# A fused attention and gated MLP kernel on one core: attention by 256-token steps over all heads in place of whole sequences by head pair

## The chip, the cores and the metric

The kernel runs on one core of a Trainium2 chip. A core has a matrix engine (TensorE, "PE" in the profile, with "PEld" for its weight loads), a vector engine (VectorE, "DVE"), a scalar engine (ScalarE, "ACT"), a general engine (GpSimd, "POOL") and a queue engine that here only issues transfers (SyncE, "SP"). Each engine works through its own list of instructions in order and waits for the others by semaphores. Data come from device memory (HBM) by 16 DMA engines into SBUF; TensorE writes to PSUM, from where VectorE or ScalarE carry results back to SBUF ("eviction"). The metric is the time of one execution in microseconds (us), lower is better.

## The reference

`x` is the attention's output with the heads side by side; shapes are batch 4, 8 heads, 768 tokens, head size 64, model width 512, MLP width 1024.

```python
# attention, for each block of 64 tokens, state kv_state (64 x 64 per head) starts at 0
intra = einsum('bhic,bhjc->bhij', qb, kb) * Dmask      # lam**(i-j) for i >= j, else 0
intra = einsum('bhij,bhjd->bhid', intra, vb)
inter = einsum('bhid,bhde->bhie', qb * lam_pow, kv_state)
out[:, :, sl] = intra + inter
kv_state = lam_block * kv_state + einsum('bhsd,bhse->bhde', kb * rev_pow, vb)
# gated MLP on x (4, 768, 512)
h = maximum(x @ w_in, 0);  u, v = h[..., :512], h[..., 512:]
v_n = (v - mean(v)) / sqrt(var(v) + 1e-6)              # over the 512 features
v_s = einsum('ts,bsd->btd', w_spatial, v_n) + b_spatial
out = (u * v_s) @ w_out
```

Inputs and output are fp32; q, k and v have 6.29 MB each, the output 6.29 MB, w_in 2.10, w_spatial 2.36, w_out 1.05 MB. Of `v_s` every token of a batch needs all 768 tokens' `v_n`, so the second half of the MLP starts when the first is done for the batch.

## The kernel before

Attention is computed in blocks of 128 tokens. The state's and the mask's powers of `lam` are put into the operands: k is cast to bf16 and scaled per head (`kd`, by `ldec`), the transposed q is scaled on eviction (`qT`, by `lq`), and the scores are scaled by a causal mask (`a`, by `amask`).

The work around attention is cut into *units*: unit u is one batch and one pair of heads (g), over all 768 tokens, 16 units in all. A unit has five parts: `cast_unit` (kd on ScalarE, qc on VectorE for batch 0 and on GpSimd after, vc on GpSimd), `trans_unit` (12 transposes into one PSUM tile `pt`, evicted as kT by ScalarE and qT by VectorE), `scores_unit` (12 matmuls into two tiles `pam`, each evicted by VectorE with the mask), `kv_unit` (10 matmuls into `pkv`, then a chain of one copy and four multiply-adds on VectorE that makes the five states `s`), and `out_unit` (10 matmuls with the state and 12 with the scores into `pat`, evicted by ScalarE into a fourth of `xT`, the MLP's transposed input).

The MLP of a batch is cut into *pieces* (`gmlp_pieces`): three `pv` (256 tokens of v each, with the normalization on VectorE), four `pu` (128 features of u, all tokens), four `pvs` (the product over tokens and the gate `gT`), three `po` (256 tokens of the output, evicted by ScalarE and stored). Since `xT` has all its rows only after the fourth unit, `pv` and `pu` of a batch come behind all four units.

All PSUM tiles come from one ring of four slots of two banks (`two_banks`), so a piece can start when the piece four places ahead of it is evicted. SBUF tiles come from pools with a number of buffers (`fin` for inputs: 2, each a whole batch).

The order on TensorE and GpSimd is that of the program text (`manual_schedule`); on the other engines a scheduler of the framework sets it when the kernel is built. The main loop interleaves: batch 0's units, then 11 of its MLP pieces; then for each further batch its units, with the pieces of the batch ahead put between them by `fill(n)`, which takes n pieces from the list `pend`. The last batch's MLP stands alone at the end.

Loads of q, k and v go through SP's queue: batch 0 by head pair (12 transfers), the others as three transfers a batch; those of batch 1 are issued at unit 2, and its k load is made to wait for the load of w_spatial (`after`). The weights are loaded by GpSimd's queue, cast to bf16 on the way. Stores of the output use SP's queue too.

Of the kernel before, what the change touches and what calls it, by code (L numbers as in the profile page):

```python
# [9 lines left out]
FP32 = mybir.dt.float32  # L10
BF16 = mybir.dt.bfloat16
# [7 lines left out]
def kernel(  # L19
# [21 lines left out]
    NU = B * NG  # L41
    HW_ = S // 2
    NPAIR = S // (2 * P)
# [3 lines left out]
    fin = ctx.enter_context(tc.tile_pool(name="fin", bufs=2))  # L47
# [4 lines left out]
    ostg = ctx.enter_context(tc.tile_pool(name="ostg", bufs=2))  # L52
# [9 lines left out]
    q_in, k_in, v_in = {}, {}, {}  # L62

    def alloc_in(b):
        q_in[b] = fin.tile([P, H, NPAIR, 2, D], FP32, tag="q_in", name=f"q_in_{b}")
        k_in[b] = fin.tile([P, H, NBLK, D], FP32, tag="k_in", name=f"k_in_{b}")
        v_in[b] = fin.tile([P, H, NBLK, D], FP32, tag="v_in", name=f"v_in_{b}")

    def load_q(b, h0, h1):
        return nc.sync.dma_start(  # L70
            out=q_in[b][:, h0:h1].rearrange("p h r m d -> p (h r) (m d)"),
            in_=q[b, h0:h1].rearrange("h (r p m) d -> p (h r) (m d)", p=P, m=2))

    def load_kv(dst, src, b, h0, h1):
        return nc.sync.dma_start(  # L75
            out=dst[b][:, h0:h1].rearrange("p h m d -> p (h m) d"),
            in_=src[b, h0:h1].rearrange("h (m p) d -> p (h m) d", p=P))

    def after(inst, gate, reason):
        tc.add_manual_dep(inst.ins, gate.ins.name,  # L80
                          mybir.DependencyInfo(mybir.DependencyClass.Sync,
                                               mybir.DependencyReason.DATA), reason=reason)

    def load_batch(b, gate=None):
        alloc_in(b)
        li = load_kv(k_in, k, b, 0, H)
        if gate is not None:
            after(li, gate, "earlier loads go first")
        load_q(b, 0, H)
        load_kv(v_in, v, b, 0, H)  # L90

    alloc_in(0)
    for g in range(NG):
        load_kv(k_in, k, 0, 2 * g, 2 * g + 2)
        load_q(0, 2 * g, 2 * g + 2)
        load_kv(v_in, v, 0, 2 * g, 2 * g + 2)
# [9 lines left out]


    qpos = iota_f([P, 2, 2, D], [[1, 2], [0, 2], [2, D]], 1, 0, "qpos")
    krev = iota_f([P, 1], [[0, 1]], P - 1, -1, "krev")
# [7 lines left out]
    wsp_raw = wpool.tile([P, NBLK, S], BF16)  # L117

# [9 lines left out]
    lq_g = []  # L128
    for g in range(NG):
        lq = const.tile([P, 2 * P], BF16, name=f"lq_{g}")  # L130
        nc.scalar.activation(out=lq, in_=qpos.rearrange("p m a d -> p (m a d)"), func=AF.Exp,
                             scale=logl[:, g:g + 1])
        lq_g.append(lq)
# [7 lines left out]
    amask = const.tile([P, H, P], FP32)  # L141
    for h in range(H):
        nc.vector.tensor_scalar(out=amask[:, h, :], in0=causal, scalar1=lm128[:, h:h + 1],
                                scalar2=None, op0=ALU.mult)
# [5 lines left out]
    def load_win(f0, f1):  # L150
        nc.gpsimd.dma_start(out=win_sb[:, :, f0:f1],
                            in_=moe_w_in.rearrange("(g p) f -> p g f", p=P)[:, :, f0:f1])


    xT = {}
    st = {}

    def cast_unit(u):
        b, g = divmod(u, NG)
        kd = att.tile([P, NBLK, 2, D], BF16, tag="kd", name=f"kd_{u}")  # L160
        qc = att.tile([P, NPAIR, 2, 2, D], BF16, tag="qc", name=f"qc_{u}")
        vc = att.tile([P, NBLK, 2, D], BF16, tag="vc", bufs=4, name=f"vc_{u}")
        for hh in range(2):
            h = 2 * g + hh
            nc.scalar.activation(out=kd[:, :, hh, :], in_=k_in[b][:, h], func=AF.Copy,  # L165
# [266 lines left out]
```

## Time and profile before

| | us |
|---|---|
| median of 3 executions | 197.62 |
| lowest, highest | 196.42, 197.75 |
| the profiled execution | 197.81 |
| its span, first to last instruction | 195.7 |

| engine | busy us | share of the span | instructions |
|---|---|---|---|
| PE | 154.7 | 79% | 1476 |
| PEld | 94.0 | 48% | 1476 |
| DVE | 103.8 | 53% | 252 |
| ACT | 94.9 | 48% | 130 |
| POOL | 31.5 | 16% | 70 |

The mean granted TensorE clock is 0.961 of full speed. The page gives the span in 40 slices of 4.89 us, a digit for the busy tenths of each engine in each; groups of instructions with their count, busy time, mean duration in ns and the idle time ahead of them with its releaser; and the DMA rate by slice. A row of a timeline has the start, the length from the first start to the last end, engine, line, operation, `out<-in`, shapes and count. Ends of matmuls are modelled, so two neighbouring rows overlap a little, and a price is best read from start to start.

### The profile page before, as it was taken

Reading aid. Unit: us, or ns where it says so; the run is one execution under the profiler, and the core shown is the slowest. Engines: PE = TensorE matmul, PEld = TensorE weight load, DVE = VectorE, ACT = ScalarE, POOL = GpSimd, SP = SyncE. Lnnn points to the kernel's source line nnn. Section 1 sums busy time; section 2 is a strip of 40 time slices with the busy share of each in tenths; the row PEclk is TensorE's granted clock in tenths of the full one; section 3 lists DMA queues with packets and bytes.
Section 4 is the critical chain, followed back from the end, with each engine's and each line's share of the span. In section 5 each row is a group of like instructions: output and inputs, shape, how many; then the busy total and the mean of one; then the engine's idle time right before and its main releaser. Section 6 shows DMA issues by size and latency. Waiting matters only on the chain.

```text
span 195.7 us, 3558 instructions
## 1 busy us (share of the span) xinstructions
PE 154.7 (79%) x1476; PEld 94.0 (48%) x1476; DVE 103.8 (53%) x252; ACT 94.9 (48%) x130; POOL 31.5 (16%) x70
## 2 busy tenths in 40 slices
PE   0046678999549999599589999976899999999980
PEld 0035565457225655355346655543566554466430
DVE  1448777094114767717995584059964830663300
ACT  3563542498463176736456542476463226670041
POOL 2124106102621015330223110030000000000000
PEclk9999999999987999859969999999999999999998
DMA  4999999999999997999910000430000005300034
GB/s 113 224 247 229 250 270 264 242 238 254 202 230 253 266 217 252 233 306 272 218 27 0 3 0 0 173 154 0 3 0 0 3 0 210 115 0 0 0 141 181
DMA packets 33151, 28.33 MB, mean 145 GB/s; under 512 B 13040, under 2 KB 27760, under 8 KB 33136
## 3 DMA queue, kind: packets, MB, share of 16 engines
q1 hardware_dynamic: 30480, 25.17, 51.7%
q0 software_dynamic: 2512, 2.95, 8.7%
q8 instruction: 11, 0.18, 0.4%
q14 instruction: 4, 0.03, 0.1%
q10 hardware_dynamic: 144, 0.00, 0.0%
HBM read 24.78 MB, written 6.29 MB: 159 GB/s over the span
## 4 chain that ended last, share of the span: by engine, by line
PE 47%; DMA 22%; DVE 13%; SPq 9%; ACT 6%; issue 2%; POOL 0%; ACTq 0%; DVEq 0%
PE pvs L303 16%; PE pu L292 8%; PE po L317 7%; DMA wsp_raw<-in_moe_w_spatial_dram 7%; DMA k_in<-in_k_dram 6%; DMA v_in<-in_v_dram 6%; SPq L75 5%; PE pv L273 4%; DVE a L214 4%; SPq L70 3%; DMA out_dram<-o 3%; PE pvs L305 3%; DVE gT L307 2%; DVE st L278 2%; PE pat L244 2%; PE pat L250 2%
## 5 line engine op out<-in xcount | busy, mean ns | idle before, releaser
L303 PE MATMUL pvs<-wt_sb,vn 128*128 128x384 bf16 x192 | 38.3, 336 | 3.2 <-ACT wt_sb L335 1.9
L253 ACT ACTIVATE xT<-pat 128x768 bf16<-128x768 f32 x16 | 16.5, 1030 | 34.5 <-PE pat L250 34.5
L214 DVE TENSOR_TENSOR a<-pam,amask 128x768 bf16<-128x768 f32 x32 | 29.4, 947 | 5.8 <-PE pam L211 5.8
L307 DVE TENSOR_TENSOR gT<-pvs,uT 128x768 bf16<-128x768 f32 x16 | 15.3, 957 | 24.7 <-PE pvs L305 24.7
L303 PEld LDWEIGHTS <-vn 128*128 128x128 bf16 x192 | 19.1, 100 | 16.1 <-issue 5.2
L292 PE MATMUL pu<-xT,win_sb 128*128 128x384 bf16 x128 | 23.6, 340 | 1.9 <-ACT xT L253 1.9
L273 PE MATMUL pv<-win_sb,xT 128*128 128x512 bf16 x96 | 24.3, 407 | 0.6 <-ACT vh L276 0.4
L171 POOL CAST vc<-v_in 128x384 bf16<-128x384 f32 x32 | 15.6, 515 | 52.2 <-DMA v_in<-in_v_dram 45.9
L278 DVE BATCH_NORM_STATS2 st<-vh 128x6 f32<-128x512 bf16 x24 | 15.7, 675 | 13.5 <-ACT vh L276 13.5
L317 PE MATMUL po<-wout_sb,gT 128*128 128x512 bf16 x96 | 21.9, 379 | 0.9 <-DVE gT L307 0.5
L190 DVE TENSOR_TENSOR qT<-pt,lq 128x768 bf16<-128x768 bf16 x16 | 8.8, 553 | 25.7 <-ACT kT L188 25.6
L320 ACT ACTIVATE o<-po 128x1024 f32<-128x1024 f32 x12 | 12.3, 1023 | 19.6 <-PE po L317 15.6
L165 ACT ACTIVATE kd<-k_in,ldec 128x384 bf16<-128x384 f32 x32 | 17.5, 603 | 7.7 <-DMA k_in<-in_k_dram 4.2
L181 PE MATMUL pt<-ident,kd 128*128 128x128 bf16 x96 | 9.6, 247 | 14.7 <-ACT kd L165 14.7
L211 PE MATMUL pam<-qT,kT 64*128 64x128 bf16 x192 | 9.4, 238 | 12.7 <-DVE qT L190 12.7
L188 ACT ACTIVATE kT<-pt 128x768 bf16<-128x768 bf16 x16 | 12.9, 807 | 12.5 <-PE pt L184 12.5
L230 DVE SCALAR_TENSOR_TENSOR s<-s,l,pkv 128x64 bf16<-128x64 bf16 x64 | 17.8, 279 | 1.8
L169 POOL CAST qc<-q_in 128x384 bf16<-128x384 f32 x24 | 11.6, 510 | 44.6 <-PE pt L184 27.4
L292 PEld LDWEIGHTS <-win_sb 128*128 128x128 bf16 x128 | 12.7, 101 | 10.8 <-issue 3.4
L276 ACT ACTIVATE vh<-pv 128x1024 bf16<-128x1024 f32 x12 | 12.3, 1022 | 9.1 <-PE pv L273 9.1
L211 PEld LDWEIGHTS <-kT 64*128 64x128 bf16 x192 | 7.3, 103 | 17.4 <-issue 9.6
L181 PEld LDWEIGHTS <-kd 128*128 128x128 bf16 x96 | 7.3, 110 | 17.3 <-ACT kd L165 15.1
(51 smaller groups left out, 155.3 us busy)
## 6 DMA issues: line engine op xcount, KB each, us to landing
out_dram<-o SPq DMA_DIRECT2D x12, 512.0 KB, 3.0
k_in<-in_k_dram SPq DMA_DIRECT2D x4, 384.0 KB, 6.4
q_in<-in_q_dram SPq DMA_DIRECT2D x4, 384.0 KB, 6.1
v_in<-in_v_dram SPq DMA_DIRECT2D x4, 384.0 KB, 6.4
wsp_raw<-in_moe_w_spatial_dram POOLq DMA_DIRECT2D x1, 1152.0 KB, 13.6
win_sb<-in_moe_w_in_dram POOLq DMA_DIRECT2D x2, 512.0 KB, 7.6
wout_sb<-in_moe_w_out_dram POOLq DMA_DIRECT2D x1, 512.0 KB, 17.2
bsp_bc<-in_moe_b_spatial_dram POOLq DMA_DIRECT2D x1, 192.0 KB, 14.1
```

The source lines that it names most:

```text
L165: nc.scalar.activation(out=kd[:, :, hh, :], in_=k_in[b][:, h], func=AF.Copy, scale=ldec[:, h:h + 1])
L181: nc.tensor.transpose(out=pk[:, m * P:(m + 1) * P], in_=kd[:, m].rearrange("p h d -> p (h d)"), identity=ident)
L211: nc.tensor.matmul(out=pam[:, hh, c, :], lhsT=kT[hh * D:(hh + 1) * D, t * P:(t + 1) * P], rhs=qblk(u, hh, t), start=True, stop=True)
L214: nc.vector.tensor_tensor(out=a_sb[:, :, 3 * i:3 * i + 3, :], in0=pam[:, :, 0:3, :], in1=amask[:, 2 * g:2 * g + 2].unsqueeze(2).broadcast_ ...
L230: nc.vector.scalar_tensor_tensor(out=s_sb[:, m], in0=s_sb[:, m - 1], scalar=l128[:, g:g + 1], in1=pkv[:, m], op0=ALU.mult, op1=ALU.add)
L253: nc.scalar.activation(out=xT[b][:, g, :].rearrange("p (c d m) -> p c m d", c=NBLK, m=2), in_=po[:, 0:NBLK].rearrange("p c (m d) -> p c m ...
L273: nc.tensor.matmul(out=ps[:, j], lhsT=x[:, c, t * P:(t + 1) * P], rhs=win_sb[:, c, DH:DFF], start=(c == 0), stop=(c == NCH - 1))
L278: nc.vector.bn_stats(out=st6[:, t, :], in_=vh[:, t, :])
L292: nc.tensor.matmul(out=ps[:, i, 0:HW_], lhsT=win_sb[:, c, f * P:(f + 1) * P], rhs=x[:, c, i * HW_:(i + 1) * HW_], start=(c == 0), stop=(c ...
L303: nc.tensor.matmul(out=ps[:, i, 0:HW_], lhsT=vn[:, s, f * P:(f + 1) * P], rhs=wt_sb[:, s, cols], start=(s == 0), stop=False)
L307: nc.vector.tensor_tensor(out=gT[:, f, :].rearrange("p (i x) -> p i x", i=2), in0=ps[:, :, 0:HW_], in1=uT[:, f, :].rearrange("p (i x) -> p ...
L317: nc.tensor.matmul(out=ps[:, j], lhsT=gT[:, c, t * P:(t + 1) * P], rhs=wout_sb[:, c, :], start=(c == 0), stop=(c == NCH - 1))
```

## The change

Attention is cut the other way. A *step* n is one batch and 256 tokens (r = 0, 1, 2 within the batch), over all eight heads, 12 steps in all. The state is carried from a step to the next through `s`, of which a step makes two (one in the last step of a batch). The first half of the MLP (`pv`, and `pu`, now 256 tokens by all features) can follow a step, and is put into `pend` by `after_out`: `pv` of each step, `pu` of step 0 at once and of the two others at the end of the batch. `pvs`, `po` and `wt_piece` (the transposes of w_spatial) are as before.

Loads are by step: two k transfers, one of q, two of v, for each step, in four buffers; the first half of w_in is loaded ahead of everything else on GpSimd's queue and w_spatial, b_spatial and w_out behind step 1's casts; no load waits for another by an added dependency. kd is made by one multiply of 1024 elements with a broadcast `ldec`, on VectorE for batch 0 and on GpSimd after; qc by one ScalarE copy.

```diff
-    fin = ctx.enter_context(tc.tile_pool(name="fin", bufs=2))
+    fin = ctx.enter_context(tc.tile_pool(name="fin", bufs=4))
...
-    ostg = ctx.enter_context(tc.tile_pool(name="ostg", bufs=2))
+    ostg = ctx.enter_context(tc.tile_pool(name="ostg", bufs=3))
...
+    def load_step(n):
+        b, r = divmod(n, NR)
+        toks = slice(r * T2, (r + 1) * T2)
...
+        for c in range(2):
+            nc.sync.dma_start(out=k_in[:, :, c, :],
+                              in_=k[b, :, toks][:, c * P:(c + 1) * P].rearrange("h p d -> p h d"))
+        nc.sync.dma_start(out=q_in.rearrange("p h m d -> p h (m d)"),
+                          in_=q[b, :, toks].rearrange("h (p m) d -> p h (m d)", m=2))
...
+    load_step(0)
...
+    load_win(DH, DFF)
+    for n in range(1, 4):
+        load_step(n)
...
+    def cast_step(n):
...
+        eng = nc.vector if n < NR else nc.gpsimd
+        eng.tensor_tensor(out=kd.rearrange("p c h d -> p h c d"), in0=s["k_in"],
+                          in1=ldec.unsqueeze(2).unsqueeze(3).broadcast_to((P, H, 2, D)),
+                          op=ALU.mult)
+        nc.scalar.activation(out=qc.rearrange("p m h d -> p h m d"), in_=s["q_in"], func=AF.Copy)
+        nc.gpsimd.tensor_copy(out=vc, in_=s["v_in"])
...
+    def kv_step(n):
...
+        for c in range(nb):
+            prev = s_sb[:, 0] if c == 1 else (st[n - 1]["s"][:, 1] if r > 0 else None)
+            if prev is None:
+                nc.vector.tensor_copy(out=s_sb[:, c], in_=pkv[:, c])
+            else:
+                sd = att.tile([P, NG, D], FP32, tag="sd", name=f"sd_{n}_{c}")
+                nc.vector.tensor_tensor(out=sd, in0=prev, in1=lb, op=ALU.mult)
+                nc.vector.tensor_tensor(out=s_sb[:, c], in0=sd, in1=pkv[:, c], op=ALU.add)
...
+    def pu(b, r):
+        x, uT = xT[b], gm[b]["uT"]
+        ps = two_banks([P, NCH, T2], f"pu_{b}_{r}")
+        for f in range(NCH):
+            for c in range(NCH):
+                nc.tensor.matmul(out=ps[:, f], lhsT=win_sb[:, c, f * P:(f + 1) * P],
+                                 rhs=x[:, r, c, :], start=(c == 0), stop=(c == NCH - 1))
...
+    def after_out(n):
+        b, r = divmod(n, NR)
+        pend.append(lambda: pv(b, r))
+        if r == 0:
+            pend.append(lambda: pu(b, 0))
+        if r == NR - 1:
+            pend.append(lambda: pu(b, 1))
+            pend.append(lambda: pu(b, 2))
+            if b == 0:
+                pend.extend([lambda s=s: wt_piece(s) for s in (0, 2, 4)])
+            pend.extend([lambda f=f: pvs(b, f) for f in range(NCH)])
+            pend.extend([lambda i=i: po(b, i) for i in range(NR)])
...
+        cast_step(0)
+        load_win(0, DH)
+        cast_step(1)
+        nc.gpsimd.dma_start(out=wsp_raw, in_=moe_w_spatial.rearrange("(a p) s -> p a s", p=P))
...
+        trans_step(0)
+        scores_step(0)
+        kv_step(0)
+        trans_step(1)
+        load_step(4)
+        fills = {0: 1, 1: 2, 2: 5}
+        for n in range(NS):
+            if n + 2 < NS:
+                cast_step(n + 2)
+            if n + 5 < NS:
+                load_step(n + 5)
+            if n + 1 < NS:
+                scores_step(n + 1)
+            out_step(n)
+            after_out(n)
+            if n + 1 < NS:
+                kv_step(n + 1)
+            f = fills.get(n, 4 + (n % 3 == 0))
+            fill(f // 2)
+            if n + 2 < NS:
+                trans_step(n + 2)
+            fill(f - f // 2)
         fill(len(pend))
```

In the rows below a name carries the batch and unit, or the step, and a number of the buffer: `kT_5_784` is kT of unit 5, `vh_1_1070` the evicted `pv` of batch 1. On ScalarE before, around the first units of batch 1 and the end of batch 0's MLP:

```order
L165 ACTIVATE kd_7_930<-k_in_1_399,ldec_126 128x6x64 x2
L188 ACTIVATE kT_5_784<-pt_5_771 128x768
L253 ACTIVATE xT_1_830<-pat_4_831 128x6x2x64
L165 ACTIVATE kd_8_1104<-k_in_2_665,ldec_126 128x6x64 x2
L320 ACTIVATE o_0_0_881<-po_0_0_872 128x1024
L188 ACTIVATE kT_6_897<-pt_6_884 128x768
```

And on ScalarE now, around steps 5 to 7 (batch 1 is steps 3 to 5):

```order
L153 ACTIVATE qc_8_1280<-q_in_8_752 128x8x2x64
L168 ACTIVATE kT_6_1054<-pt_6_1037 128x1024
L325 ACTIVATE o_0_2_1067<-po_0_2_1058 128x1024
L280 ACTIVATE vh_1_1070<-pv_1_0_1077 128x1024
L252 ACTIVATE xT_1_781<-pat_5_1130 128x8x2x64
L153 ACTIVATE qc_9_1469<-q_in_9_937 128x8x2x64
L284 ACTIVATE rstd_1_1076<-mv_1_1075,eps_t_166 128x2
L299 ACTIVATE uT_1_1072<-pu_1_0_1186 128x4x256
L280 ACTIVATE vh_1_1070<-pv_1_1_1204 128x1024
L168 ACTIVATE kT_7_1239<-pt_7_1222 128x1024
```

Before, the copies that stand two or three units ahead read a batch that was loaded whole; now they read the load of a step two or three steps ahead, and evictions of earlier steps stand behind them. On SP before, from the loads of batch 2 on:

```order
L75 DMA v_in_2_666<-in_v_dram 128x48x64
L321 DMA out_0_dram<-o_0_0_881 128x2x512
L321 DMA out_0_dram<-o_0_1_910 128x2x512
L75 DMA k_in_3_1099<-in_k_dram 128x48x64
L321 DMA out_0_dram<-o_0_2_989 128x2x512
L70 DMA q_in_3_1098<-in_q_dram 128x24x128
```

And on SP now, from the load of step 9 (batch 3 is steps 9 to 11):

```order
L74 DMA q_in_9_937<-in_q_dram 128x8x128
L77 DMA v_in_9_939<-in_v_dram 128x8x64 x2
L326 DMA out_0_dram<-o_0_0_1022 128x2x512
L326 DMA out_0_dram<-o_0_1_1034 128x2x512
L326 DMA out_0_dram<-o_0_2_1067 128x2x512
L72 DMA k_in_10_1102<-in_k_dram 128x8x64 x2
L74 DMA q_in_10_1101<-in_q_dram 128x8x128
```

Before, two of batch 0's three stores stood ahead of the last batch's k load; now all three stand ahead of the loads of the last two steps, and the loads of all other steps stand ahead of the stores.

415 lines of the change are left out of this document (164 added, 251 removed).

## The prediction

> **What bounds the kernel now.** I read the page first (busy shares and the forty slices of 4.89 us), then the busy time by stages, then TensorE in order of time.
>
> ```profile
> span 195.7 us, 3558 instructions
> PE   0046678999549999599589999976899999999980
> DVE  1448777094114767717995584059964830663300
> DMA  4999999999999997999910000430000005300034
> GB/s 113 224 247 229 250 270 264 242 238 254 202 230 253 266 217 252 233 306 272 218 27 0 3 0 0 173 154 0 3 0 0 3 0 210 115 0 0 0 141 181
> ```
>
> Two kernels stand one behind the other. Up to slice 20 (98 us) the DMA engines are full and TensorE has holes; from there on TensorE is full but for dips where DVE stands at 9. Loads bound the first third, TensorE the rest, DVE its dips.
>
> ```profile
> 34.90:56.70 21.80, 16.34 (x109) 8.96 (x107) 7.98 (x22) 14.23 (x18) 5.47 (x12) 1.00 1.10 234
> 56.70:126.00 69.30, 62.05 (x650) 37.48 (x651) 41.51 (x92) 36.05 (x51) 15.31 (x32) 0.90 0.66 158
> 164.65:184.13 19.48, 19.48 (x114) 10.96 (x112) 9.45 (x24) 7.99 (x11) 0.00 (x0) 1.00 0.15 56
> 184.13:195.70 11.57, 5.52 (x25) 2.17 (x23) 0.96 (x1) 3.07 (x3) 0.00 (x0) 0.93 0.35 136
> 90.00:100.00 10.00, 6.84 (x76) 3.98 (x75) 9.59 (x28) 6.21 (x11) 1.01 (x3) 0.92 0.95 197
> 130.00:140.00 10.00, 7.29 (x92) 4.46 (x90) 9.96 (x28) 5.67 (x9) 0.00 (x0) 1.00 0.05 19
> ```
>
> (Columns: stretch, its length, busy us of PE, PEld, DVE, ACT, POOL, granted clock, DMA share, GB/s.) With the MLP alone (164.65 to 184.13) TensorE has no gap. In the two ten-us rows three `pv` pieces in a row come with attention, DVE is at 9.59 and 9.96, and TensorE loses 3.16 and 2.71 us.
>
> **Prices.** TensorE undisturbed, start to start:
>
> ```profile
> 46.30 2.17 PE L332 MATMUL pwt<-ident,wsp_raw 128*128 128x128 bf16 x36
> 56.69 0.51 PE L181 MATMUL pt<-ident,kd 128*128 128x128 bf16 x6 [3.52 <-ACT kd L165]
> ...
> 143.91 0.51 PE L211 MATMUL pam<-qT,kT 64*128 64x128 bf16 x12 [0.22 <-DVE qT L190]
> 144.35 0.47 PE L244 MATMUL pat<-qT,s 64*64 64x128 bf16 x10
> 144.74 0.53 PE L250 MATMUL pat<-a,vc 128*64 128x128 bf16 x12
> 145.10 0.32 PE L225 MATMUL pkv<-vc,kd 128*64 128x64 bf16 x10
> 145.36 1.47 PE L292 MATMUL pu<-xT,win_sb 128*128 128x384 bf16 x8
> ...
> 148.94 0.50 PE L181 MATMUL pt<-ident,kd 128*128 128x128 bf16 x6
> 149.28 0.50 PE L184 MATMUL pt<-ident,qc 128*128 128x128 bf16 x6
> 149.61 1.14 PE L303 MATMUL pvs<-wt_sb,vn 128*128 128x384 bf16 x6
> ...
> 159.46 5.35 PE L317 MATMUL po<-wout_sb,gT 128*128 128x512 bf16 x24
> 164.65 5.34 PE L273 MATMUL pv<-win_sb,xT 128*128 128x512 bf16 x24
> 169.83 5.36 PE L292 MATMUL pu<-xT,win_sb 128*128 128x384 bf16 x32
> 175.03 1.14 PE L303 MATMUL pvs<-wt_sb,vn 128*128 128x384 bf16 x6
> ...
> 184.13 0.81 PE L317 MATMUL po<-wout_sb,gT 128*128 128x512 bf16 x3
> ```
>
> A unit: pam 0.44, pat 0.39 + 0.36, pkv 0.26, pt 2 x 0.34; 2.13, a batch of four 8.5. A step issues 16 of each kind instead of 12 or 10: pt 0.91, pam 0.59, pat 0.62 + 0.48, pkv 0.42, so 3.02; the first step of a batch saves 8 `pat` (0.31), the last 8 `pkv` (0.21); a batch 8.5. The same work. MLP of a batch: po 5.19, pv 5.18, pu 5.20, pvs 9.10, sum 24.7; `pu` in 48 of 256 columns instead of 32 of 384 has the same columns (nearest row: 384 columns at 0.163), taken at 1.73 a piece. All: 4 x 33.2 + 2.2 (pwt) = 135.0 us. The change removes no TensorE work; what it can save are holes.
>
> **Where before stands.** At 56.69 all of batch 0 but three `pvs` (6.8) and `po` (5.2) is done; 111.6 us are left, 106.4 of them ahead of the last `po`, which starts at 184.13: 127.4 - 106.4 = 21.0 us lost.
>
> **Where the change stands.** Step data is 1.57 MB, either half of w_in 0.52 as written, the rest of the weights 1.9 (shapes). Summing the GB/s row (2.1 MB at 11.6 us, 4.2 at 20.4, 6.3 at 28.5, 8.7 at 38.0, 12.4 at 53.8): step 0 and the first w_in half are in at 11.6 (that half now goes ahead), step 1 at 20.4, then wsp, b_spatial and w_out share the engines with step 2, whose q is in at 28.5; q of step 3 at 38.0. TensorE: step 2's transposes at 29.7 and `pv` behind them at about half speed, as after each pause in these rows:
>
> ```profile
> 34.92 6.34 PE L273 MATMUL pv<-win_sb,xT 128*128 128x512 bf16 x24
> 57.37 2.05 PE L303 MATMUL pvs<-wt_sb,vn 128*128 128x384 bf16 x6
> ```
>
> (pvs 2.05 against 1.14 later.) So until 34.9, then pam, pat, pkv, pu (3.6) to 38.5; the transposes of step 3 wait for the q copy and end at 40.3. That is the last long wait for a load. Done by then: 2.7 + 3.0 + 1.7 + 0.9 of attention, one `pv`, one `pu`: 11.8 us. Left ahead of the last `po`: 135.0 - 11.8 - 5.2 = 118.0, so it would start at 158.3, and 11.6 us later (row 184.13:195.70, unchanged) the span ends: 169.9 with no further loss.
>
> **Losses.** Other engines:
>
> ```profile
> L214 DVE TENSOR_TENSOR a<-pam,amask 128x768 bf16<-128x768 f32 x32 | 29.4, 947 | 5.8 <-PE pam L211 5.8
> L190 DVE TENSOR_TENSOR qT<-pt,lq 128x768 bf16<-128x768 bf16 x16 | 8.8, 553 | 25.7 <-ACT kT L188 25.6
> L230 DVE SCALAR_TENSOR_TENSOR s<-s,l,pkv 128x64 bf16<-128x64 bf16 x64 | 17.8, 279 | 1.8
> L171 POOL CAST vc<-v_in 128x384 bf16<-128x384 f32 x32 | 15.6, 515 | 52.2 <-DMA v_in<-in_v_dram 45.9
> L165 ACT ACTIVATE kd<-k_in,ldec 128x384 bf16<-128x384 f32 x32 | 17.5, 603 | 7.7 <-DMA k_in<-in_k_dram 4.2
> L253 ACT ACTIVATE xT<-pat 128x768 bf16<-128x768 f32 x16 | 16.5, 1030 | 34.5 <-PE pat L250 34.5
> L320 ACT ACTIVATE o<-po 128x1024 f32<-128x1024 f32 x12 | 12.3, 1023 | 19.6 <-PE po L317 15.6
> ```
>
> - Eviction of `a` and `qT` by 1024 instead of 768 elements, 24 and 12 times instead of 32 and 16: the same elements, eight and four fixed parts fewer. No cost; TensorE has two to five other pieces to cover them, where a unit had one or two.
> - The state: 20 small operations a batch of 0.28 become one copy, four multiplies and four adds of 256 elements, none in the trace; between 0.28 (the small one) and 0.55 (qT, 768) I take 0.4, 3.6 us a batch instead of 5.3.
> - Casts: kd (32 of 603 ns) leaves ACT, qc comes: 12 of 1024 elements, between 1.02 (o) and 1.6 (kd scaled); about even. Three kd go to DVE, bounded by 0.95 and 1.5, in a stage that waits for loads. Nine kd go to POOL, multiply by a broadcast: bounds 1.37 (cast scaled) and twice that, 2.7; two inputs stand nearer to two casts, so I take 2.5, with vc 1.4 that is 3.9 of the 11 us of a step, covered by the load lead; if it were 10 us POOL would pace the steps.
> - wt_sb: the third `pwt` stands right ahead of `pvs`, whose fifth matmul needs its ACT copy: 1.1 us (bounds 0 and 1.5).
> - DVE: three `pv` are spread over a step and a half, not ten us; I take half the loss of the rows at 90 and 130, 1.5 us, for three batches 4.5 (bounds 0 and 9).
> - ACT: the q copy of step n+3 stands ahead of evictions of step n+1, and ACT is in order. For step 9 it stands ahead of rstd, uT, vh, kT. By the prices 35.4 us of TensorE work lie between 40.3 and the end of `pat` of step 5, with the 1.1 above that is 76.8, and xT takes 1.3 (1030 ns for 768, scaled): ACT gets there at 78.1. The q of step 9 is in after 18.2 MB, 77.3 us, or 83.9 if batch 0's output (1.57 MB) goes first. The late case stops TensorE for the slot of uT and then for kT: 3.8 us. I take 2.0 (bounds 0 and 3.8).
> - SP: the loads of steps 10 and 11 stand behind batch 0's outputs, which wait for `po` (about 75 us). The q of step 10 is then in after 21.3 MB, about 89 us, and ACT reaches its copy at about 92. Nothing, with 3 us to spare; without them up to a step's load, 6.6.
> - End: `pvs` of batch 3 waits for the last vn, 1.0 (bounds 0 and 2).
>
> Sum 8.6 us: span 178.5. The profiled execution of 195.7 took 197.81, 2.1 more, and lies 0.2 above the median of 197.62: 180.6, say **181**.
>
> **The rivals.** *The holes stay*: DVE and ACT work is unchanged in sum, and if TensorE loses per unit of work what it lost before, 21.0 x 118.0/106.4 = 23.3, the span is 193.2, the time 195.3. For it: 9.96 of 10 busy on DVE. Against: part of the 21.0 is half speed after pauses for loads (clock 0.90 in 56.70:126), which no longer come there.
>
> *No further loss, head 3 us sooner*: 169.9 + 2.1 = 172.
>
> *Loads by step are slower*: 60 load issues in place of 21, of 256 and 512 KB, where those of batches 1 to 3 have 1.5 MB. Steps 0 and 1 with w_in are in at 20.4, 1.9 MB of weights take 7.5 (250 GB/s), and if each of ten more steps takes x us, step 11 is in at 27.9 + 10x. Behind that TensorE has, in its order: casts 2.0, pt 0.9, three pvs 6.8, pam, pat and pkv 1.9, po and pv 6.9, pat 1.1, five pv and pu 8.6, pvs 9.1, end 11.6, together 48.9. It decides above x = 12.1 us (130 GB/s), where the time passes 199.6. Against: the slices with 384 KB loads (2 to 5) moved 224 to 250 GB/s, x = 6.6, the leanest full one 202. If the five loads of a step went one after the other, each with a fixed part, x = 13.6 is within reach: 27.9 + 136 + 48.9 + 2.1 = 215. The Trainium skill, DMA: Bandwidth & Descriptors, section Bandwidth, speaks for that: it wants transfers of 1 MiB or more for 75% of peak and gives 2.0 us plus bytes over 436 GB/s for one, an estimate of 13.6 us for the five. By that rule the time is 215; the trace does not agree as long as several are in flight (234 GB/s and full engines with 384 KB loads).
>
> **How the numbers follow.** Forecast 0.65 (own range 176 to 187); no loss 0.12; holes stay 0.13; slow loads 0.10. A measurement of this kernel can tell about 1% from no change. Faster by over 1% (below 195.6): the first two and half of the third, 0.83; within 1%: 0.07; slower: 0.10. The range 172 to 194 leaves out the slow loads, the worse half of the third and a little below: about 0.8.
>
> **What would show it.** Right: DMA slices full at 220 to 270 GB/s; step 3's transposes near 40 us; then no TensorE slice below 8 until the end; 11.6 us from last `pvs` to the end; POOL's kd below 3 us. Wrong: q loads past their q copy on ACT in steps 5 to 9, DVE at 9.9 with TensorE at 7 in each batch, full-rate slices below 200 GB/s, a granted clock below 0.9 past 60 us.

## The result and the profile after

| | before | after |
|---|---|---|
| median | 197.69 us (196.42 to 198.13) | 187.77 us (187.36 to 188.46), 4 runs each |
| ratio to before | 1 | 0.9512, 95% interval 0.9459 to 0.9565 |
| profiled execution: time, span | 197.81 us, 195.7 us | 188.46 us, 186.7 us |

The change makes the kernel 4.9% faster. The forecast was 181.0 us with a range of 172 to 194. The gain is there, but it is 6.8 us smaller than forecast. Here and below, medians are over all executions, while ratios and their intervals leave out those that lie over 1.5% above the fastest of the same kernel.

From the page of the profile after, the span, the slices (4.67 us each) of TensorE, VectorE and the DMA engines, the GB/s, and the queue that SyncE's loads and stores go through (packets, MB, share of 16 engines):

```profile
span 186.7 us, 3638 instructions
PE   0005677507979779999997999999799999999980
DVE  1029993705399853542989747169884722564400
DMA  4999969999999999999998900530000027000035
GB/s 98 218 211 252 205 161 184 199 212 232 199 241 248 200 239 238 221 225 222 330 254 195 252 8 0 208 133 4 0 0 4 2 79 262 0 0 4 0 132 205
q1 hardware_dynamic: 65664, 25.17, 56.5%
```

Read it from the right. From slice 15 (70 us) TensorE is at 9 but for two slices at 7, where before it fell to 5 and 6 in the same stretch: the holes in the middle are mostly closed. On the left there is a whole slice of 0 (slice 8, 37 to 42 us) while the DMA engines are full. The GB/s row has 161 to 199 in slices 5 to 7, where before had 242 to 270; in slice 5 the engines were not full (digit 6), in slices 6 and 7 they were.

TensorE around that hole and at the two other places that matter, in order of time (start, duration, what; in brackets the idle time ahead and who ended it):

```profile
43.09 0.43 PE L207 MATMUL pkv<-vc,kd 128*64 128x64 bf16 x8 [8.07 <-POOL vc L154]
43.45 3.54 PE L297 MATMUL pu<-xT,win_sb 128*128 128x256 bf16 x16
...
47.27 0.61 PE L163 MATMUL pt<-ident,qc 128*128 128x128 bf16 x8
47.72 1.89 PE L277 MATMUL pv<-win_sb,xT 128*128 128x512 bf16 x8
...
66.49 0.48 PE L307 MATMUL pvs<-wt_sb,vn 128*128 128x384 bf16 x2 [1.96 <-ACT wt_sb L336]
66.81 0.32 PE L309 MATMUL pvs<-bsp_bc,oo 128*128 128x384 bf16 x1
66.97 1.81 PE L307 MATMUL pvs<-wt_sb,vn 128*128 128x384 bf16 x6
...
175.54 0.81 PE L322 MATMUL po<-wout_sb,gT 128*128 128x512 bf16 x3
```

The transposes of step 3, which the forecast had ending at 40.3 us, end at 47.7 (the start of the next row; for the experiments below, the modelled end is given, which here is 0.2 later). From there the same 118.0 us of work stand ahead of the last `po` as the forecast counted; it starts at 175.54, so 127.8 - 118.0 = 9.8 us are lost (forecast 8.6). The end takes 186.7 - 175.54 = 11.2 us (forecast 11.6). So the span misses the 178.5 forecast by 7.4 + 1.2 - 0.4 = 8.2 us, and the start is nearly all of it.

The same bill against before: there 106.4 us were left at 56.69, which without loss ends at 163.1; after, 118.0 at 47.72, which ends at 165.7. So the start of the changed kernel is 2.6 us *worse* than before's. Losses fall from 21.0 to 9.8 us, the end gives 0.4, and 11.2 + 0.4 - 2.6 = 9.0 us is the difference of the spans.

What the hole waits for stands in the rows of SyncE's and GpSimd's queues:

```profile
25.44 0.83 POOL L362 DMA_DIRECT2D wsp_raw<-in_moe_w_spatial_dram  x1
26.26 0.56 POOL L363 DMA_DIRECT2D bsp_bc<-in_moe_b_spatial_dram  x1
26.81 0.76 POOL L364 DMA_DIRECT2D wout_sb<-in_moe_w_out_dram  x1
42.00 1.04 POOL L154 CAST vc<-v_in 128x1024 bf16<-128x1024 f32 x1 [14.43 <-DMA v_in<-in_v_dram]
...
24.29 2.20 SPq L77 DMA_DIRECT2D v_in<-in_v_dram  x2
26.54 10.03 SPq L72 DMA_DIRECT2D k_in<-in_k_dram  x2
36.61 5.17 SPq L74 DMA_DIRECT2D q_in<-in_q_dram  x1
```

v of step 2 is issued at 24.29, the three weights right beside it, and v lands only just before 42.0. SyncE then needs 10.03 us to issue k of step 3, two instructions that take 1.1 to 5.5 us in the other steps up to 75 us, and 5.17 for q. That the weights hold up the step loads is a reading so far; the experiments test it.

One part of this start belongs to this profile. Four runs below have the same loads up to here (projections first, transposes earlier, projections by batch, ScalarE's order written out). They move 228 to 231 GB/s between 20 and 29 us and end step 3's transposes at 44.6 to 45.8. The profile of the changed kernel moves 180 in that stretch, with a DMA share of 0.82 instead of 1.13 to 1.20; first its row, then that of the transposes earlier (columns as in the prediction; the last two are the DMA share and GB/s):

```profile
20.00:29.00 9.00, 5.13 (x78) 4.29 (x76) 8.44 (x14) 3.15 (x3) 3.11 (x4) 1.00 0.82 180
```

```profile
20.00:29.00 9.00, 5.05 (x85) 4.60 (x84) 8.60 (x14) 3.40 (x3) 3.11 (x4) 0.73 1.13 228
```

Why it is so, and whether the other three executions of the changed kernel have it, stays open; their spans are 0.5 to 1.1 us shorter.

### The profile page after: what moved, and what is told of

It reads as the page before. It is cut to its first block, busy times and chain, and to the rows that moved or that the text cites. A ratio compares the mean times of both kernels' runs of the same rounds, so it can differ in the third digit from the quotient of the medians.

```text
span 186.7 us, 3638 instructions
## 1 busy us (share of the span) xinstructions
PE 145.7 (78%) x1540; PEld 96.5 (52%) x1540; DVE 103.4 (55%) x191; ACT 89.1 (48%) x98; POOL 34.8 (19%) x35
## 3 DMA queue, kind: packets, MB, share of 16 engines
q1 hardware_dynamic: 65664, 25.17, 56.5%
## 4 chain that ended last, share of the span: by engine, by line
PE 54%; SPq 13%; DVE 11%; ACT 9%; DMA 9%; issue 2%; POOL 1%; ACTq 0%; POOLq 0%
PE pvs L307 17%; PE po L322 11%; DMA v_in<-in_v_dram 9%; PE pv L277 8%; PE pu L297 7%; SPq L77 6%; SPq L72 5%; PE pt L163 4%; DVE a L192 3%; PE pvs L309 3%; SPq L74 3%; DVE st L282 3%; ACT vh L280 2%; ACT wt_sb L336 2%; DVE vn L288 2%
## 5 line engine op out<-in xcount | busy, mean ns | idle before, releaser
L192 DVE TENSOR_TENSOR a<-pam,amask 128x1024 bf16<-128x1024 f32 x24 | 28.5, 1210 | 6.0 <-PE pam L189 6.0
L154 POOL CAST vc<-v_in 128x1024 bf16<-128x1024 f32 x12 | 12.9, 1074 | 84.0 <-DMA v_in<-in_v_dram 42.7
L252 ACT ACTIVATE xT<-pat 128x1024 bf16<-128x1024 f32 x12 | 15.8, 1320 | 23.7 <-PE pat L249 23.6
L297 PE MATMUL pu<-xT,win_sb 128*128 128x256 bf16 x192 | 24.4, 285 | 1.9 <-DVE a L192 1.9
L153 ACT ACTIVATE qc<-q_in 128x1024 bf16<-128x1024 f32 x12 | 12.7, 1055 | 19.0 <-DMA q_in<-in_q_dram 19.0
L150 POOL TENSOR_TENSOR kd<-k_in,ldec 128x1024 bf16<-128x1024 f32 x9 | 17.1, 1897 | 6.1 <-DMA k_in<-in_k_dram 6.1
L168 ACT ACTIVATE kT<-pt 128x1024 bf16<-128x1024 bf16 x12 | 12.2, 1021 | 11.2 <-PE pt L163 11.2
L280 ACT ACTIVATE vh<-pv 128x1024 bf16<-128x1024 f32 x12 | 12.3, 1024 | 8.8 <-PE pv L277 8.8
L277 PEld LDWEIGHTS <-xT 128*128 128x128 bf16 x96 | 9.5, 102 | 11.7 <-issue 1.7
L322 PEld LDWEIGHTS <-gT 128*128 128x128 bf16 x96 | 9.2, 98 | 11.9 <-issue 1.0
L299 ACT ACTIVATE uT<-pu 128x1024 bf16<-128x1024 f32 x12 | 12.2, 1020 | 5.9 <-PE pu L297 5.8
```

The costliest lines, as they stand in the source:

```text
L150: eng.tensor_tensor(out=kd.rearrange("p c h d -> p h c d"), in0=s["k_in"], in1=ldec.unsqueeze(2).unsqueeze(3).broadcast_to((P, H, 2, D)), ...
L154: nc.gpsimd.tensor_copy(out=vc, in_=s["v_in"])
L192: nc.vector.tensor_tensor(out=a_sb[:, i].rearrange("p h g c x -> p (h g) c x"), in0=pam.rearrange("p h g c x -> p (h g) c x"), in1=amask[: ...
L252: nc.scalar.activation(out=xT[b][:, r].rearrange("p g (c d m) -> p (g c) m d", c=2, m=2), in_=po.rearrange("p g c (m d) -> p (g c) m d", m ...
L277: nc.tensor.matmul(out=ps[:, j], lhsT=x[:, r, c, j * P:(j + 1) * P], rhs=win_sb[:, c, DH:DFF], start=(c == 0), stop=(c == NCH - 1))
L280: nc.scalar.activation(out=vh[:, pair, :], in_=ps, func=AF.Relu)
```

## Experiments on the start: what holds up step 2 and step 3

All experiments start from the changed kernel. Times are medians beside runs of before on the same chip; where those runs differ from 197.7 us, the ratio is the fairer measure (the changed kernel's is 0.9512). The code is shown shortened; words in brackets say where a line stands.

**All three weights later.** They are issued behind step 2's casts instead of step 1's.

```diff
-        wsp_raw, bsp_bc, wout_sb loads          (behind cast_step(1))
+            if n == 0: wsp_raw, bsp_bc, wout_sb loads   (behind cast_step(n + 2))
```

> The loads of w_spatial, b_spatial and w_out are issued by GpSimd one step later, behind the casts of step 2 instead of step 1. Theory A (these weights, 1.9 MB as written, take the engines from step 2's v, which landed at 42.0 us where the sum had 33.7): v of step 2 lands by 34 us, the wait of 8.1 us ahead of step 2's state matmuls is below 2 us, step 3's transposes end at 40 to 43 us, the median is 181 to 185 us unless the late weights stop the first pvs by more than 3 us. Theory B (loads in 256-byte packets are slow by themselves, about 200 GB/s): v of step 2 lands later than 38 us, the median stays between 186 and 189.5.

190.40 us (188.55 to 192.01), ratio 0.9628 (0.9448 to 0.9808). TensorE, SyncE's queue and ScalarE:

```profile
35.09 0.61 PE L163 MATMUL pt<-ident,kd 128*128 128x128 bf16 x8
37.24 0.62 PE L163 MATMUL pt<-ident,qc 128*128 128x128 bf16 x8 [1.55 <-ACT qc L153]
...
46.81 0.64 PE L207 MATMUL pkv<-vc,kd 128*64 128x64 bf16 x16 [5.27 <-POOL vc L154]
53.02 0.61 PE L277 MATMUL pv<-win_sb,xT 128*128 128x512 bf16 x1 [5.57 <-ACT xT L252]
...
24.07 3.87 SPq L72 DMA_DIRECT2D k_in<-in_k_dram  x2
31.75 9.91 SPq L72 DMA_DIRECT2D k_in<-in_k_dram  x2
...
50.72 1.06 ACT L153 ACTIVATE qc<-q_in 128x1024 bf16<-128x1024 f32 x1 [10.06 <-DMA q_in<-in_q_dram]
51.68 1.29 ACT L252 ACTIVATE xT<-pat 128x1024 bf16<-128x1024 f32 x1
```

The wait of 8.07 us is gone, and the transposes of step 3 end at 37.9, ahead of theory A's 40 to 43; the time lies above both ranges. The 10-us issue is now that of step 4's k (31.75), and TensorE waits 5.27 us for v of step 3. The slow issue has followed the weights, so they cause it. The other wait, 5.57 us, has a second cause: on ScalarE the q copy of step 4 now stands ahead of `xT` of step 2, whose `pat` is done by 41.5, while in the changed kernel that `xT` (51.58) stands ahead of the copy (52.95). So this run does not show what the later weights alone are worth; had these 5.57 us reached the end, the estimate is 185 us, within theory A.

**Projections of step 0 ahead of step 2's kv work**, so that TensorE has something to do in the hole.

```diff
+            if n == 1: fill(f)                  (ahead of kv_step(n + 1))
-            fill(f // 2); trans_step(n + 2); fill(f - f // 2)
+            if n != 1: fill(f // 2) ... fill(f - f // 2)
```

> In iteration 1 the two MLP pieces (pu of step 0, pv of step 1) stand ahead of step 2's state matmuls, which wait for v of step 2, instead of behind them. Theory (the 8.1 us wait there is on the path, and work that needs no load can stand in it): 3.5 us of TensorE work and the half speed behind the pause leave the path, median 182 to 185. Rival (loads bound the stage; the transposes of steps 3 and 4 wait instead): within 1% of the changed kernel, 186 to 189.5.

187.55 us (186.57 to 189.29), ratio 0.9524 (0.9359 to 0.9689): no change. The work fits into the hole, and behind it TensorE stands 5.99 us at `43.44` for k of step 3. The hole was not a matter of TensorE's order alone.

**w_out alone later**, from behind step 1's casts to behind step 4's, 0.5 MB less beside the loads of steps 2 and 3.

```diff
-        nc.gpsimd.dma_start(out=wout_sb, ...)   (behind cast_step(1))
+            if n == 2: nc.gpsimd.dma_start(out=wout_sb, ...)
```

> Only the load of w_out goes from behind step 1's casts to behind step 4's; the spatial weights and bias stay. Theory R (bytes ahead of the steps set the landing): w_out's bytes at some 205 GB/s are 2 to 3 us that the v of step 2 and k, v of step 3 come sooner, transposes of steps 3 and 4 end 2 us sooner, 184.5 to 187 us. Rival, that w_out was not what the steps waited behind: the same waits at the same times, 187 to 189 us.

184.07 us (182.94 to 184.65), ratio 0.9287 (0.9225 to 0.9350), below the changed kernel's interval. The wait of 8.07 us is gone, and what comes in its place is shorter, 4.50 us for k of step 3:

```profile
34.49 0.29 PE L207 MATMUL pkv<-vc,kd 128*64 128x64 bf16 x8
34.71 1.92 PE L297 MATMUL pu<-xT,win_sb 128*128 128x256 bf16 x16
41.13 1.04 PE L163 MATMUL pt<-ident,kd 128*128 128x128 bf16 x8 [4.50 <-POOL kd L150]
41.96 1.06 PE L163 MATMUL pt<-ident,qc 128*128 128x128 bf16 x8
...
63.94 0.48 PE L307 MATMUL pvs<-wt_sb,vn 128*128 128x384 bf16 x2 [1.96 <-ACT wt_sb L336]
64.43 1.14 PE L307 MATMUL pvs<-wt_sb,vn 128*128 128x384 bf16 x6
```

Step 3's transposes end at 43.0 instead of 47.7, and the span is 4.2 us shorter. w_out is not needed before `po` of batch 0 at 79.8; it had been put in the one stage that loads bound. Not all of the 4.7 us is proved to be w_out's: the 180 instead of 231 GB/s between 20 and 29 us are 0.46 MB or 2 us, and they lie mostly ahead of w_out's issue. Against the four other profiles with the same loads, step 3 is 1.6 to 2.8 us earlier. The gain in time rests on the ratios, whose intervals lie apart.

**w_in's halves behind steps 0 and 1**, instead of ahead of and behind step 0.

```diff
-    load_win(DH, DFF)                           (ahead of the loads of steps 1 to 3)
         cast_step(0)
-        load_win(0, DH)
+        load_win(DH, DFF)
         cast_step(1)
+        load_win(0, DH)
```

> The first half of w_in is issued behind step 0's casts and the second behind step 1's, instead of ahead of step 0's and behind it. Theory R: q, k, v of step 0 land sooner and TensorE starts at 11 to 12 us instead of 14.3, but the wait goes to the first projection or to the v of step 2, transposes of step 3 still end at 46.5 to 48.5, 186 to 189 us. Rival, that the late start is what delays the rest: the start's 2 to 3 us come off the end, 184 to 186 us.

185.91 us (184.70 to 188.50), ratio 0.9373 (0.9313 to 0.9432). TensorE starts at 10.0 us instead of 14.3, but waits 9.45 us for k of step 3, whose transposes end at 45.1. Of the 4.3 us some 2 reach the end, where the two expectations meet. The order of bytes can be shifted in this stage; half of it is paid back three steps later.

**Packets of 512 bytes.** k and v go in runs of two tokens, in as many transfers and bytes.

```diff
-            dma k_in[:, :, c, :] <- k[b, :, toks][:, c * P:(c + 1) * P]    "h p d -> p h d"
+            dma k_in[:, hs]      <- k[b, hs, toks]     "h (p m) d -> p h (m d)", m=2
```

> k and v of a step are loaded in 512-byte runs (two tokens of a head in a row), in as many transfers and bytes as before; rows of keys then belong to other tokens, so the output is not the reference's. Theory P, that the 256-byte packets make a step's loads slow: the GB/s row in slices 3 to 12 rises from a mean of about 205 to 230 or more, the v of step 2 has landed by 39 us instead of 42, step 3's transposes have ended by 45 us instead of 47.7, and the kernel takes 182 to 185 us. Rival R, that it is the amount loaded ahead of it, with the weights in between, at a rate that packets don't set: GB/s and landing as in the changed kernel, 186 to 189 us.

192.81 us (192.62 to 193.05), ratio 0.9742 (0.9698 to 0.9787): slower than the changed kernel, which neither theory said. The page shows that the rate did rise, and ScalarE and TensorE show what went wrong:

```profile
GB/s 82 255 298 262 282 216 215 281 290 290 295 278 295 292 276 291 269 8 287 157 3 2 3 0 0 102 230 3 0 0 3 0 13 317 4 0 3 0 119 210
q1 hardware_dynamic: 41088, 25.17, 47.6%
```

```profile
39.01 1.06 ACT L155 ACTIVATE qc<-q_in 128x1024 bf16<-128x1024 f32 x1 [12.90 <-DMA q_in<-in_q_dram]
...
41.31 3.59 PE L279 MATMUL pv<-win_sb,xT 128*128 128x512 bf16 x8 [9.65 <-ACT xT L254]
```

Loads run mostly at 260 to 298 GB/s (slices of 4.78 us), at 215 beside the weights, and are through by 96 us instead of 107. But with other loads the scheduler ordered ScalarE otherwise: the q copy of step 3 stands ahead of `xT` of step 0, which in the changed kernel stands ahead even of step 2's copy. ScalarE works in order, so `xT`, and TensorE behind it (9.65 us), wait for a load that neither needs. So the time of this run says nothing on the packets; its rate and its landings do.

**ScalarE's order written out**, with 256-byte and with 512-byte runs, so that only the packets differ.

```diff
-    with tc.manual_schedule(engines={PE, Pool}):
+    with tc.manual_schedule(engines={PE, Pool, Activation}):
+            q_copy(n + 2)                       (behind out_step(n), not in cast_step)
-        eng = nc.vector if n < NR else nc.gpsimd
+        eng = nc.vector if n < 2 else nc.gpsimd
```

> The changed kernel with ScalarE's order written out too: each step's q copy behind the eviction of the attention output two steps before it, as the changed kernel has it for steps 2 to 4, and the decay product of step 2 on GpSimd instead of VectorE. It is the base for the next run. Loads as in the changed kernel (some 210 GB/s up to 56 us): step 3's transposes end at 45 to 49, 186 to 191 us; copies that now stand ahead of later evictions in other places may cost or save a microsecond or two.

> The same with k and v loaded in 512-byte runs (rows of keys belong to other tokens, so the output is not the reference's); ScalarE's order is the same in both. Theory P with its order fault taken out: the loads run at 270 GB/s or more as in the run with 512-byte runs alone, step 3's transposes end by 42 us, and the kernel takes 5 to 8 us less than with ScalarE's order alone, 179 to 184 us. Rival, that the rate is not what the head waits for: within 2 us of the run with ScalarE's order alone.

199.76 us (198.28 to 201.72) and 196.13 us (195.01 to 197.28). As a base this is poor: writing the order out by hand cost 12 us (ratios 1.0146, 1.0010 to 1.0283, and 1.0018, 0.9972 to 1.0063). In the second one's rows of ScalarE one cause is seen: `rstd` waits 1.57 to 3.05 us for VectorE's statistics, and in five of twelve places `xT` stands right behind it. Whether that is all of the 12 us is not shown.

```profile
49.67 0.29 ACT L290 ACTIVATE rstd<-mv,eps_t 128x2 f32<-128x2 f32 x1 [3.05 <-DVE mv L289]
49.87 1.29 ACT L258 ACTIVATE xT<-pat 128x1024 bf16<-128x1024 f32 x1
```

Between the two, GpSimd's rows for v of step 2 and k of step 3, first with 256, then with 512 bytes:

```profile
38.18 1.04 POOL L158 CAST vc<-v_in 128x1024 bf16<-128x1024 f32 x1 [12.44 <-DMA v_in<-in_v_dram]
40.12 1.90 POOL L153 TENSOR_TENSOR kd<-k_in,ldec 128x1024 bf16<-128x1024 f32 x1 [0.91 <-DMA k_in<-in_k_dram]
```

```profile
30.63 1.04 POOL L160 CAST vc<-v_in 128x1024 bf16<-128x1024 f32 x1 [6.21 <-DMA v_in<-in_v_dram]
37.75 1.90 POOL L155 TENSOR_TENSOR kd<-k_in,ldec 128x1024 bf16<-128x1024 f32 x1 [6.08 <-DMA k_in<-in_k_dram]
```

v comes 7.6 us sooner and k, which decides, 2.4 us; the kernel takes 3.6 us less, and no run of one lies among those of the other, though the intervals of the ratios touch. That is less than the 5 to 8 expected and more than the rival's 2: the packets matter, by about half of what I thought, and only 2.4 of the 3.6 us are seen at the start.

## Experiments on the losses behind it

**The spatial weights' transposes earlier**, ahead of the first batch's last two `pu`.

```diff
+            if b == 0: pend.extend(wt_piece(0), wt_piece(2), wt_piece(4))
             pend.append(pu(b, 1)); pend.append(pu(b, 2))
-            if b == 0: pend.extend(wt_piece(0), wt_piece(2), wt_piece(4))
```

> The three pieces that transpose w_spatial stand ahead of the last two pu pieces of batch 0, not behind them. Theory (the first pvs waits 2.0 us for the third ScalarE copy, and the pause sets TensorE to half speed for some 3 us more): the 2.0 us go and the pvs and pt rows behind run at full speed, median 183.5 to 186. Rival (the pause costs its own 2 us at most, the rest of it is taken by vn or by the next load): 186 to 188.

186.47 us (182.93 to 187.44), beside a median of before of 199.27 there. The spread is too wide to tell the two expectations apart by time, and there is no ratio for it. The profiled execution is the fastest of these, so its span is not compared. In its rows the first `pvs` has no wait and full speed:

```profile
60.22 1.92 PE L297 MATMUL pu<-xT,win_sb 128*128 128x256 bf16 x16
61.97 1.14 PE L307 MATMUL pvs<-wt_sb,vn 128*128 128x384 bf16 x6
```

Of the 3.8 us that the copy costs in the changed kernel (below), 0.94 stay, ahead of a `pat`.

**Projections by batch again**, everything else as changed: `pv` and `pu` of a batch are all queued behind its third step.

```diff
-        pend.append(pv(b, r))
-        if r == 0: pend.append(pu(b, 0))
         if r == NR - 1:
-            pend.append(pu(b, 1)); pend.append(pu(b, 2))
+            pend.extend(pv(b, 0..2)); pend.extend(pu(b, 0..2))
```

> Undoes one part: pv and pu of a batch are put into the list only when its three steps are done, as before the change; steps, loads and the number of pieces taken per step stay. Theory (the gain over the kernel before comes from pieces of MLP at every step, so that no pause follows the transposes and the three pv do not pile up on VectorE): most of the gain goes, 192 to 198. Rival (the gain comes from the steps and their loads): 186 to 189.5.

193.95 us (193.75 to 194.24), ratio 0.9836 (0.9709 to 0.9962). By the same bill: transposes of step 3 end at 45.8 with one `pv` and one `pu` (3.5 us) less behind them, so 121.5 us are left, and the last `po` starts at 181.32: 14.0 us lost instead of 9.8, and a start 1.6 us worse. That is the 5.8 us between the spans (192.5 and 186.7). So of the 9.9 us that the change brings, some 6 come from the projections right behind each step; the rest is left for the steps of all heads and their loads, by subtraction. Where the 6 us are lost can be told from the bill, too. At 87.47, behind batch 0's first `po`, 89.5 us of work are left ahead of the last `po`, so 4.3 us are lost from there on; the changed kernel, with 92.2 left at 79.82, loses 3.5. So some 5 of the 5.8 us come before the second batch's projections, where loads bound and TensorE has no other pieces. The theory's other half, that three `pv` in a row pile up on VectorE, is not borne out: later in this run TensorE is nearly full with VectorE below 8 (columns as in the prediction).

```profile
130.00:140.00 10.00, 9.58 (x113) 6.33 (x113) 7.92 (x19) 6.74 (x9) 0.00 (x0) 1.00 0.22 81
```

**Three edits together**: projections first, transposes earlier, w_out later.

> Three edits together: projections of step 0 all ahead of step 2's kv work, the spatial weights' transposes ahead of the first batch's last projections, w_out's load behind step 4's casts. If the gains lie in different places (the copy behind the transposes and the half speed there some 4 us, the landing of steps 2 and 3 some 2): 180 to 184 us. If the loads still bound the first four steps, only the middle edit counts: 184 to 187 us.

184.00 us (183.27 to 184.55), ratio 0.9294 (0.9246 to 0.9342), as w_out alone, on the border of the two expectations. The gain behind the weights' copy is there in the rows (no wait, `pvs` at 62.92 in 1.14 us). But TensorE now stands 1.90 us ahead of `pam` at 44.86 and 1.75 ahead of `pv` at 50.06, which then takes 3.58 us; with w_out alone there is no wait at that `pam`, 1.15 at that `pv`, and it takes 1.90. The pieces moved forward are missing there.

**More of the MLP in iteration 2**, on top of the three edits: ten pieces instead of five, and w_out behind step 3's casts instead of step 4's.

```diff
-        fills = {0: 1, 1: 2, 2: 5}
+        fills = {0: 1, 1: 2, 2: 10}
```

> As the three edits together, with two more: in iteration 2 ten pieces of the MLP are emitted instead of five, so that the first batch's spatial product stands ahead of step 4's output instead of behind step 4's kv work, and w_out is loaded behind step 3's casts. Theory R (loads set when steps 3 and 4 can go on, and TensorE only lacks work that needs no further load): the 8 us of the spatial product go into the idle time that stands between 36 and 58 us, the span falls by 3 to 6 us against the three edits' 182.1, the kernel takes 177 to 181 us. Rival, that idle time there is a chain of vector and scalar work and not the loads, so that the product only waits in its turn: 182 to 186 us.

190.57 us (189.00 to 192.41), ratio 0.9657 (0.9483 to 0.9832): worse than both expectations. The spatial product does not get into the hole, since step 2's own projections stand ahead of it; it runs from 61.5 to 70.7. And the pieces that it uses up are missing later, where TensorE then waits with nothing to do:

```profile
85.71 1.90 PE L277 MATMUL pv<-win_sb,xT 128*128 128x512 bf16 x7 [1.29 <-ACT xT L252]
...
90.70 0.62 PE L189 MATMUL pam<-qT,kT 64*128 64x128 bf16 x16 [2.19 <-DVE qT L170]
...
93.88 1.90 PE L277 MATMUL pv<-win_sb,xT 128*128 128x512 bf16 x7 [1.17 <-ACT xT L252]
```

**The three single gains together**: w_in behind steps 0 and 1, w_out behind step 4, transposes earlier.

> Three edits that were each tried alone, in three different places: w_in's halves behind step 0's and step 1's casts (1.9 us less than the changed kernel's median), w_out behind step 4's casts (3.7 us less), the spatial weights' transposes ahead of the first batch's last projections (1.3 us less). If the places are apart: step 3's transposes end by 43 us, no wait of 2 us for the spatial weights' copy, 180 to 183 us. If the first two are one gain (both make the same load sooner), and the third is what the three edits before showed: 183 to 185 us.

182.28 us (180.63 to 183.75, 6 runs), ratio 0.9234 (0.9171 to 0.9297). This beats before by 7.7% and the changed kernel by 2.9% (the ratios divided). Step 3's transposes end at 42.2 and the wait of 1.96 us is gone, yet the single gains (1.9, 3.7 and an uncertain 1.3 us) do not add up to 6.9 but to 5.5: v of step 2 still holds TensorE for 5.88 us. Against w_out alone the intervals overlap.

## The prediction, step by step

- *The time*: 187.8 us lies in the stated range, but 0.8 above the forecast branch's own 176 to 187. Holes were saved, as it said. One landing was far off, and the reason given for the VectorE term is not borne out (both below).
- *TensorE's work is unchanged, holes are what can be saved*: right. Losses went from 21.0 to 9.8 us. That this is near the forecast's 8.6 is partly luck: two terms came out 2.7 and 1.2 us larger (wt_sb, and a wait for `xT` that was not foreseen), three others 1.1, 2.0 and 0.5 smaller.
- *"The transposes of step 3 ... end at 40.3. That is the last long wait for a load"*: the place is right, the size is the step that failed. It measured 47.7. The forecast took the landing from the GB/s row of before: 8.7 MB by 38.0 us, 229 GB/s. The q of step 3 came at 45.6, and the row of after sums to 9.0 MB by then: the amount was right, the rate was 196. The row of before was no price for other loads beside the weights. With 512-byte runs the same sum reaches 9.0 MB at 38.1 us, so the forecast landing comes back with the packets; with w_out moved away the landmark comes to 43.0. Some 2 to 3 of the 7.4 us are this profile's (44.6 to 45.8 in the four others with the same loads). How the rest divides between packets and weights isn't settled, since each of them changes what the other costs.
- *wt_sb, 1.1 us*: mis-sized. Waits of 0.26 and 1.96 us, and about 1.6 because TensorE runs at half speed behind the pause (from 66.97 `pvs` in 1.81 instead of 1.14; the granted clock is 0.54 from 66.97 to 70.60): 3.8. The forecast had seen half speed after pauses and charged it only to load waits. But half speed does not follow this pause each time: with w_out later, w_in behind, and ScalarE's order written out (both runs), the same wait of 1.96 to 1.98 us is followed by `pvs` in 1.14 us (the last rows of w_out later). So the copy costs 2.2 us in these, and 3.8 in the profile of the changed kernel.
- *VectorE, 4.5 us*: 3.4 us (0.94 and 0.93 for an `a`, 0.37 ahead of three `po`, 0.41 for `qT`). Its rows at the places of those shown of before, and the end:

```profile
90.00:100.00 10.00, 9.38 (x119) 6.76 (x117) 9.29 (x24) 7.93 (x11) 2.87 (x3) 1.00 1.08 273
130.00:140.00 10.00, 9.07 (x123) 7.07 (x121) 8.51 (x21) 4.78 (x7) 0.00 (x0) 1.00 0.00 0
...
175.54:186.70 11.16, 5.52 (x26) 2.17 (x23) 0.96 (x1) 3.07 (x3) 0.00 (x0) 1.00 0.37 141
```

VectorE (the fifth number) was at 9.59 and 9.96 and is at 9.29 and 8.51, TensorE at 9.38 and 9.07 instead of 6.84 and 7.29. But the reason given for it, that the three `pv` are spread, is not borne out: with projections by batch TensorE is at 9.63 and 9.58 in these stretches and VectorE at 7.28 and 7.92. So the loss went with the attention by steps, whose part in it no run takes apart.

- *q copies ahead of evictions on ScalarE, 2.0 us*: nothing in steps 7 to 11. The mechanism is real all the same: it cost TensorE 9.65 us in one place with 512-byte runs, and 5.57 us with all three weights later. *The last vn, 1.0 us*: 0.5. Not foreseen: a `pv` that waits 1.16 us for `xT` at 52.95.
- *Prices*: `kd` on GpSimd 1897 ns (2500 taken), `vc` 1074 (1400), `kd` on VectorE 1221 (0.95 to 1.5), and for the state 415 for the sum, 396 for the copy and 573 for `sd` (400 taken for each).
- *The rivals*: no further loss fell, at 9.8 us lost (its 172 us is the sum without losses; the 3 us of its name are not in it). Holes stay fell as far as losses go. Loads by step slower did not decide: behind the weights a step's load takes 6.6 to 7.7 us (SyncE's k issues of 43.94, 50.87, 57.50, 65.21 and 72.63), near the 6.6 named and far from 12.1 (by its own sum it passes the forecast of 181 from 10.2 on). With several in flight, transfers of 256 and 512 KB moved 199 to 248 GB/s in slices 7 to 18, so the 215 us, with five loads of a step one after the other, did not come. The price of one transfer behind it, 2.0 us plus bytes over 436 GB/s, stands in the Trainium skill, DMA: Bandwidth & Descriptors, section Anatomy of one DMA — SWDGE (gpsimd) path, as measured on loads that GpSimd issues; it is no price of a step here. The same page's rule of 1 MiB or more for 75% of peak (section Bandwidth) finds no support in these rows: before's slices, with loads of 1.5 MB, stay at 306 GB/s or less, and the one slice above 75% of 436 is slice 19 of after, 330 GB/s, with transfers of 512 KB or less. Beside the weights the step loads were slower, which the rival did not price apart.
- *The signs*: of those named for being wrong, three came: full-rate slices below 200 GB/s (184 and 199), a granted clock of 0.89 from 60 to 75 us, and a q load past its copy in step 7 (2.78 us on ScalarE, without a wait on TensorE). Of those for being right, `kd` below 3 us on GpSimd and the end of 11.2 us came; the rate and the place of step 3 did not, and two TensorE slices stand at 7.

## What to carry to other kernels

A landing time read from an old profile's GB/s row holds only for the same packets beside the same other loads: ask what the new loads' packets cost, and keep out of the load-bound stage every weight that is needed later. When a wait for a load is taken away, ask what the next step waits for; where bytes bound the stage, the wait can move on. Where a scheduler sets an in-order engine's sequence, a change to the loads alone can put a copy that waits ahead of an eviction that is due.

## What the hardware showed that was not expected

Packet size: SyncE's queue kept 16 engines busy for 56.5% of 186.7 us = 105.5 us with 65664 packets, and for 47.6% of 191.2 = 91.0 us with 41088, for the same 25.17 MB. The difference of 14.5 us falls on the 12.6 MB of k and v; if the 91.0 us are spread evenly over all bytes (45.5 us for k and v), 256-byte runs cost 32% more than 512-byte ones. The other runs bear the direction out: the queue's share times the span is 103.5 to 110.2 us in those with 256-byte runs, and 90.1 us in the other with 512. Before has a third value, 51.7% of 195.7 = 101.2 us:

```profile
q1 hardware_dynamic: 30480, 25.17, 51.7%
```

Its k and v are runs of 256 bytes too, but in batches 1 to 3 they travel in larger packets (9.4 MB in packets of 256 bytes would be 36864 alone). So it is not settled how much of the 14.5 us is the packet's and how much the run's.

The Trainium skill (DMA: Bandwidth & Descriptors, section Why small descriptors are slow (HBM only)) counts 3 cycles on top of 8 for 256 bytes; by that count 512 bytes take 19, and the estimate is 16% more. It names a second cost as well, 32 bytes of metadata for each operation, which this estimate leaves out. The direction agrees, the runs show about twice the 16%.

VectorE beside GpSimd. In the changed kernel, `sd` alone and beside GpSimd's multiply:

```profile
63.98 0.42 DVE L218 TENSOR_TENSOR sd<-s,l 128x256 f32<-128x256 bf16 x1
64.89 2.14 DVE L218 TENSOR_TENSOR sd<-s,l 128x256 f32<-128x256 bf16 x1
...
64.85 1.90 POOL L150 TENSOR_TENSOR kd<-k_in,ldec 128x1024 bf16<-128x1024 f32 x1 [0.78 <-DMA k_in<-in_k_dram]
```

The second `sd` starts 0.04 us behind the multiply and ends 0.28 behind it, five times as long. `vn` does the same (2.09 us for two at 44.09 beside the multiply of 43.81, instead of 0.73 at 54.68), while statistics and the evictions from PSUM keep their time (at 51.36 the statistics take 1.27, beside a multiply too). The Trainium skill (SBUF — State Buffer, section Who interferes with whom) says that a VectorE instruction with two SBUF inputs waits for a GpSimd instruction that reads SBUF, for the whole of it; the rows of `sd` agree. `vn` has one tile as input, so that sentence does not speak of it, and why it is slow there stays open. It cost little here: no row of TensorE waits for `sd` or `s` in the changed kernel.
